# Two 64-row matmuls for the third input block's low pass, in the up-projection tiles of 512 columns

## The chip, the core and the metric

The kernel runs on one core of one Trainium2 chip. The metric is device time in microseconds (us), the median of several executions. Lower is better.

## The reference: what is computed

A gated recurrent attention runs over 4 batches, 8 heads and 768 positions of head size 40. Its output, 3072 rows of 320 values, goes through a gated feed-forward layer:

```python
x = np.ascontiguousarray(attn_out.transpose(0, 2, 1, 3)).reshape(B * S, H * D)   # 3072 x 320
gate = 1.0 / (1.0 + np.exp(-(x @ w_gate)))     # w_gate: 320 x 1536
val = x @ w_val                                # w_val:  320 x 1536
return (gate * val @ w_out).astype(np.float32) # w_out:  1536 x 320
```

The change sits in the two products `x @ w_gate` and `x @ w_val`, called the up-projection here.

## The kernel before

**The chunks.** The 768 positions are worked in six chunks of 128. A chunk holds 128 positions of each of the four batches, so 512 rows of `x`. In the kernel these are the columns of a transposed `x` with the 320 features on the partitions.

**High and low parts.** The matmuls run in the type fp32r, which keeps fewer bits than fp32. Each operand is therefore split into a high part (rounded to fp32r) and a low part (what is left): `xh` and `xl` for the input, `wh` and `wl` for the weights. A product is the sum of three passes: high times high, low weight times high input, high weight times low input.

**The three input blocks.** The 320 features make two blocks of 128 partitions and a third of 64. For the third block the kernel writes the 64 features twice, in partitions 0 to 63 and again in 64 to 127 (`twice`). Its weights lie in a tile `w2[n]`, n = 0 for the gate and 1 for the value: 64 partitions (`HP[n]`) hold the high part and the other 64 the low part. The high part of the gate is in partitions 0 to 63, that of the value in 64 to 127. One matmul of 128 rows with `w2[n]` then adds high and low weight times the input at once. It is done twice, with `xh` and with `xl`, for each of gate and value.

**A tile of the up-projection.** `ffn_up(n)` makes one tile: 128 of the 1536 output features, and either all 512 columns of the chunk (41 tiles) or 256 of them (62 tiles). It issues 16 matmuls, eight into the PSUM bank `pg0` (gate) and eight into `pg1` (value). The last two are the third block's passes with `xl`: first into `pg0`, then into `pg1`. In the text below they are called A and B. After that ScalarE takes tanh of `pg0` (line 811), VectorE multiplies with `pg1` (line 814), and two more operations (818, 822) split the product into `gh` and `gl`. The next tile's first matmul writes `pg0` again and so waits until the tanh has read it. `ffn_down` (line 833) multiplies `gh` and `gl` with the output weights into PSUM tiles `po`.

**The order of the work.** A long table of words written by hand, `ORDER`, sets the order in which every instruction is issued. The word `t27` issues the next of the 16 matmul steps of tile 27, `p26` the next down-projection matmul of tile 26, `a`, `b`, `s`, `c` and others steps of the attention. Each engine takes its instructions in the order issued.

**Where the matmul array is divided.** Most matmuls use the array whole, 128 rows by 128 columns. Two kinds do not. Line 599, `by_columns`, multiplies the score matrix with the values in four column strips of 32 (`av`, 64 instructions in a row for each batch of a chunk). Line 317 transposes gate values that lie in 32 partitions, and so uses 32 rows (`pt_h`, `pt_k`).

Of the kernel before, what the change touches and what calls it, by code (L numbers as in the profile page):

```python
# [178 lines left out]
def mlstm_then_gated_ffn_kernel(  # L179
# [13 lines left out]
    nc = tc.nc  # L193
    B, H, S, D = q.shape
    P = 128
    L = P
# [8 lines left out]
    def E(name, c=0):  # L205
        x = PARAM["eng"].get(name, "p")
        return nc.gpsimd if x == "p" else nc.vector
# [35 lines left out]
    def put(key, f, *args):  # L243
        todo.setdefault(key, []).append((f, args))
# [144 lines left out]
    wh, wl, w2 = [], [], []  # L389
# [7 lines left out]
    HP = (slice(0, 64), slice(64, P))  # L397
# [97 lines left out]
    xh, xl = {}, {}  # L495
# [286 lines left out]
    def ffn_up(n):  # L782
        c, j, t0, t1 = tiles[n]
        n0, n1 = t0 * L, t1 * L
        nt = n1 - n0
        u = (c, j, t0)
        fs = slice(j * P, (j + 1) * P)
        pg, sg = {}, []
        if n in PARAM['wllate']:
            order = [(x, i) for x in range(2) for i in (0, 2)] + [(0, 1), (1, 1)]  # L790
        else:
            order = [(x, i) for x in range(2) for i in (0, 1, 2)]

        def mm(x, w, y, a):
            first = x not in pg
            if first:
                pg[x] = ps_o.tile([P, NT], F32, tag=f"pg{x}", name=f"pg{x}_{c}_{j}_{t0}")[:, :nt]
            nc.tensor.matmul(pg[x], w[:, a, fs] if a < 2 else w[:, fs], y[c][:, a, n0:n1],  # L798
                             start=first, stop=a == 2 and y is xl)

        for x, i in order:
            w, y = ((wh, xh), (wl, xh), (wh, xl))[i]
            for a in range(2):
                put(f"t{n}", mm, x, w[x], y, a)
        for y in (xh, xl):
            for x in range(2):
                put(f"t{n}", mm, x, w2[x], y, 2)

        def tanh():
            sg.append(two.tile([P, NT], F32, tag="sg", name=f"sg_{c}_{j}_{t0}", bufs=1)[:, :nt])  # L810
            nc.scalar.activation(sg[0], pg[0], AF.Tanh, scale=0.5)  # L811

        def gate():
            nc.vector.scalar_tensor_tensor(sg[0], sg[0], 1.0, pg[1], ALU.add, ALU.mult)  # L814

        def high():
            gh[u] = two.tile([P, NT], F32R, tag="gh", name=f"gh_{c}_{j}_{t0}")
            nc.scalar.activation(gh[u][:, :nt], sg[0], AF.Copy)  # L818

        def low():  # L820
            gl[u] = two.tile([P, NT], F32R, tag="gl", name=f"gl_{c}_{j}_{t0}")
            E('gl0' if c == 0 else 'gl').tensor_tensor(gl[u][:, :nt], sg[0], gh[u][:, :nt].bitcast(F32), ALU.subtract)  # L822

        for key, f in (("ta", tanh), ("tg", gate), ("th", high), ("tl", low)):
            put(f"{key}{n}", f)
# [171 lines left out]
    for u in range(NU):  # L997
        c, b = divmod(u, B)
# [60 lines left out]
```

## Time and profile before

| | |
|---|---|
| median of 3 runs | 541.68 us (541.53 to 541.98) |
| the profiled execution | 541.76 us |
| its span, first to last instruction | 540.0 us |
| TensorE matmuls (PE) | busy 519.3 us, 4739 instructions |
| TensorE weight loads (PEld) | busy 469.3 us |
| VectorE (DVE) | busy 317.7 us |
| ScalarE (ACT) | busy 230.2 us |
| GpSimd (POOL) | busy 163.3 us |
| granted TensorE clock, mean | 0.99 |

PE and PEld are two sides of the same engine: every matmul is preceded by a load of its stationary operand, and the load can run while an earlier matmul streams. Matmuls overlap in the record: each row gives a start and a length that includes the pipeline, so the length of one (402 ns for 512 columns) is longer than the distance from its start to the next start. The distance between starts is what a matmul costs in a stream. In a timeline row such as `104.83 0.63 PE ... x2`, two matmuls stand in one row: the first starts at 104.83 us, and the end of the second is 0.63 us later. In a row of the chain of work, `310.43 3.26 PE pg L798 x14`, the second number is the time for which these 14 instructions were what the end waited for.

### The profile page before, as it was taken

Reading aid. Unit: us, or ns where it says so; the run is one execution under the profiler, and the core shown is the slowest. Engines: PE = TensorE matmul, PEld = TensorE weight load, DVE = VectorE, ACT = ScalarE, POOL = GpSimd, SP = SyncE. Lnnn points to the kernel's source line nnn. Section 1 sums busy time; section 2 is a strip of 40 time slices with the busy share of each in tenths; the row PEclk is TensorE's granted clock in tenths of the full one; section 3 lists DMA queues with packets and bytes.
Section 4 is the critical chain, followed back from the end, with each engine's and each line's share of the span. In section 5 each row is a group of like instructions: output and inputs, shape, how many; then the busy total and the mean of one; then the engine's idle time right before and its main releaser. Section 6 shows DMA issues by size and latency. Waiting matters only on the chain.

```text
span 540.0 us, 12183 instructions
## 1 busy us (share of the span) xinstructions
PE 519.3 (96%) x4739; PEld 469.3 (87%) x4739; DVE 317.7 (59%) x739; ACT 230.2 (43%) x581; POOL 163.3 (30%) x231
## 2 busy tenths in 40 slices
PE   8756999999999999999999999999999999999997
PEld 7545988888999999998888888888888888999996
DVE  5979798877655655545656645455744444543322
ACT  4676768563633443434333443243432422132322
POOL 5767667465330252040304341115210310000000
PEclk9879999999999999999999999999999999999999
DMA  9998877133596848377488385685287444000000
GB/s 196 222 258 201 220 202 184 60 85 74 143 190 174 195 99 169 78 203 152 106 182 166 74 219 146 149 193 126 58 215 185 105 107 120 25 26 1 25 1 24
DMA packets 131648, 72.41 MB, mean 134 GB/s; under 512 B 103112, under 2 KB 120776, under 8 KB 131592
## 3 DMA queue, kind: packets, MB, share of 16 engines
q1 hardware_dynamic: 130504, 71.39, 55.6%
q8 instruction: 37, 0.61, 0.5%
q10 hardware_dynamic: 1088, 0.26, 0.3%
q14 instruction: 19, 0.16, 0.1%
HBM read 56.95 MB, written 14.68 MB: 133 GB/s over the span
## 4 chain that ended last, share of the span: by engine, by line
PE 84%; DMA 6%; DVE 4%; SPq 3%; ACT 1%; issue 1%; POOL 0%; DVEq 0%; POOLq 0%; ACTq 0%
PE pg L798 48%; PE po L833 22%; PE av L599 3%; DMA qs<-scr 3%; PE pt L508 3%; PE s L629 2%; PE in L650 2%; PE cs L751 2%; PE s L624 1%; PE xt L719 1%; DMA st_o<-in_moe_w_out_dram 1%; DVE gl L822 1%; SPq L255 1%; DMA q<-in_q_dram 1%; DMA scr<-warm 1%
## 5 line engine op out<-in xcount | busy, mean ns | idle before, releaser
L798 PE MATMUL pg<-xh,wh 128*128 128x256 f32 (+1 forms) x412 | 112.3, 339 | 5.0 <-ACT sg L811 4.7
L811 ACT ACTIVATE sg<-pg 128x256 f32<-128x256 f32 (+1 forms) x103 | 48.2, 468 | 149.9 <-PE pg L798 146.8
L798 PE MATMUL pg<-xh,wl 128*128 128x256 f32 (+1 forms) x412 | 110.9, 336 | 0.0
L798 PE MATMUL pg<-xl,wh 128*128 128x256 f32 (+1 forms) x412 | 109.3, 335 | 0.0
L814 DVE SCALAR_TENSOR_TENSOR sg<-sg,pg 128x256 f32<-128x256 f32 (+1 forms) x103 | 54.0, 524 | 90.5 <-ACT sg L811 68.3
L833 PE MATMUL po<-oh,gl 128*128 128x320 f32 x288 | 90.8, 318 | 0.5 <-DVE gl L822 0.5
L833 PE MATMUL po<-oh,gh 128*128 128x320 f32 x288 | 91.0, 319 | 0.1
L833 PE MATMUL po<-ol,gh 128*128 128x320 f32 x288 | 90.6, 317 | 0.0
L822 DVE TENSOR_TENSOR gl<-sg,gh 128x256 fp32r<-128x256 f32 (+1 forms) x103 | 64.7, 628 | 27.6 <-ACT gh L818 27.4
L798 PEld LDWEIGHTS pg<-xh,wh 128*128 128x128 f32 x412 | 70.6, 191 | 10.9 <-ACT sg L811 6.6
L818 ACT ACTIVATE gh<-sg 128x256 fp32r<-128x256 f32 (+1 forms) x103 | 51.7, 502 | 58.3 <-DVE sg L814 55.7
L798 PEld LDWEIGHTS pg<-xl,wh 128*128 128x128 f32 x412 | 69.6, 191 | 4.7
L798 PEld LDWEIGHTS pg<-xh,wl 128*128 128x128 f32 x412 | 69.8, 191 | 4.4
L798 PE MATMUL pg<-xl,w 128*128 128x256 f32 (+1 forms) x206 | 58.5, 329 | 0.0
L833 PEld LDWEIGHTS po<-oh,gl 128*128 128x128 f32 x288 | 54.0, 188 | 3.9 <-DVE gl L822 0.9
L833 PEld LDWEIGHTS po<-oh,gh 128*128 128x128 f32 x288 | 54.3, 189 | 2.7 <-ACT gh L818 0.4
L833 PEld LDWEIGHTS po<-ol,gh 128*128 128x128 f32 x288 | 54.1, 188 | 2.9
L798 PE MATMUL pg<-xh,w 128*128 128x256 f32 (+1 forms) x206 | 53.3, 333 | 0.0
L702 POOL COPY x<-x 128x64 f32<-128x64 f32 x22 | 6.2, 280 | 153.8 <-DVE x L697 132.0
L635 DVE TENSOR_TENSOR d<-s,d 128x384 f32<-128x384 f32 (+1 forms) x66 | 32.9, 508 | 29.6 <-PE s L629 29.0
L367 POOL TENSOR_TENSOR d<-at,d 128x1024 f32<-128x1024 f32 x16 | 30.6, 1914 | 28.1 <-DMA d<-mscr 28.0
L798 PEld LDWEIGHTS pg<-xl,w 128*128 128x128 f32 x206 | 36.2, 189 | 2.2
(129 smaller groups left out, 776.4 us busy)
## 6 DMA issues: line engine op xcount, KB each, us to landing
d<-mscr SPq DMA_DIRECT2D x22, 512.0 KB
ks<-scr SPq DMA_DIRECT2D x16, 360.0 KB
qs<-scr SPq DMA_DIRECT2D x16, 360.0 KB
k<-in_k_dram SPq DMA_DIRECT2D x24, 160.0 KB
o<-in_o_gate_dram SPq DMA_DIRECT2D x24, 160.0 KB
v<-in_v_dram SPq DMA_DIRECT2D x24, 160.0 KB
st_o<-in_moe_w_out_dram SPq DMA_DIRECT2D x12, 320.0 KB
out_dram<-ob SPq DMA_DIRECT2D x24, 160.0 KB
```

The source lines that it names most:

```text
L367: E(arg).tensor_tensor(d, a, d, ALU.subtract)
L508: nc.tensor.transpose(pt[g][:r, x, :], t[u][:, h0 : h0 + nh, :].rearrange("p h d -> p (h d)"), ident)
L599: nc.tensor.matmul(dst[xs], lhs[:, xs], rhs, start=True, stop=True)
L629: nc.tensor.matmul(ps[g][:, m, :], ks[: 3 * D, 3 * m + g, :], qs[: 3 * D, 3 * m + g, :], start=True, stop=True)
L635: nc.vector.tensor_tensor(x, ps[g][:, :nh, :], x, ALU.mult)
L650: nc.tensor.matmul(pi[:, h0 : h0 + nh, :], qk[u][:r, g, :], cst[:r, b, g, : nh * DA], start=True, stop=True)
L798: nc.tensor.matmul(pg[x], w[:, a, fs] if a < 2 else w[:, fs], y[c][:, a, n0:n1], start=first, stop=a == 2 and y is xl)
L811: nc.scalar.activation(sg[0], pg[0], AF.Tanh, scale=0.5)
L814: nc.vector.scalar_tensor_tensor(sg[0], sg[0], 1.0, pg[1], ALU.add, ALU.mult)
L818: nc.scalar.activation(gh[u][:, :nt], sg[0], AF.Copy)
L822: E('gl0' if c == 0 else 'gl').tensor_tensor(gl[u][:, :nt], sg[0], gh[u][:, :nt].bitcast(F32), ALU.subtract)
L833: nc.tensor.matmul(po[t], g[c, j, t0][:, (t - t0) * P : (t - t0 + 1) * P], o[:, j, :], start=j == 0 and first, stop=j == NF - 1 and last)
```

## The change

In the 512-column tiles, and there alone, A and B become matmuls of 64 rows. A multiplies the high part of the gate's third block, which is in partitions 0 to 63, with the copy of `xl` in the same partitions. B does that for the value in partitions 64 to 127. Both are issued one behind the other at the step where A stood. The step where B stood issues nothing. The product of low weight and low input, which the 128-row matmuls had added too, is left out. Tiles of 256 columns stay as they were.

```diff
@@ ffn_up, mm(x, w, y, a): x is 0 for the gate and 1 for the value
             if first:
                 pg[x] = ps_o.tile([P, NT], F32, tag=f"pg{x}", name=f"pg{x}_{c}_{j}_{t0}")[:, :nt]
+            if a == 2 and y is xl and nt > 2 * L:
+                for z in range(2) if x == 0 else ():
+                    nc.tensor.matmul(pg[z], w2[z][HP[z], fs], y[c][HP[z], a, n0:n1], start=False, stop=True)
+                return
             nc.tensor.matmul(pg[x], w[:, a, fs] if a < 2 else w[:, fs], y[c][:, a, n0:n1],
                              start=first, stop=a == 2 and y is xl)
```

In the order of the instructions only TensorE's queue changes. In 20 of the 41 tiles A and B stood side by side before and still do; in 21 other work stood between them.

The first place is on TensorE in chunk 0, tile 5, at about 84 us of the span. `pg_0_5_0` with the larger number is `pg1`, with the smaller `pg0`; `w_100` and `w_103` are `w2[0]` and `w2[1]`, `xl_420` the low input. Before:

```order
L798 MATMUL pg_0_5_0_1257<-xh_398,w_103 128x512
L798 MATMUL pg_0_5_0_1223<-xl_420,w_100 128x512
L508 MATMUL pt_1_1_1291<-ident,q_1_560 80x128
L508 MATMUL pt_1_1_1291<-ident,k_1_717 80x128
L798 MATMUL pg_0_5_0_1257<-xl_420,w_103 128x512
L317 MATMUL pt_k__1295<-ident,gin 128x32 x4
```

With the change:

```order
L802 MATMUL pg_0_5_0_1257<-xh_398,w_103 128x512
L800 MATMUL pg_0_5_0_1223<-xl_420,w_100 128x512
L800 MATMUL pg_0_5_0_1257<-xl_420,w_103 128x512
L508 MATMUL pt_1_1_1292<-ident,q_1_560 80x128
L508 MATMUL pt_1_1_1292<-ident,k_1_717 80x128
L317 MATMUL pt_k__1295<-ident,gin 128x32 x4
```

B moved ahead of two transposes and stands behind A.

The second place is on TensorE in chunk 2, tile 11 of that chunk, at about 299 us, where the column strips of `av` follow. `s` are score matmuls, `po` the down-projection. Before:

```order
L798 MATMUL pg_2_11_0_4227<-xh_2567,w_103 128x512
L798 MATMUL pg_2_11_0_4213<-xl_2581,w_100 128x512
L629 MATMUL s_3_3_4256<-qs_3_4155,ks_3_4113 128x128 x2
L833 MATMUL po_2_3334<-oh,gh_10_0_4220 128x320
L798 MATMUL pg_2_11_0_4227<-xl_2581,w_103 128x512
L599 MATMUL av_3_4265<-v_3_3787,d_3_3785 32x41 x32
```

With the change:

```order
L802 MATMUL pg_2_11_0_4227<-xh_2567,w_103 128x512
L800 MATMUL pg_2_11_0_4213<-xl_2581,w_100 128x512
L800 MATMUL pg_2_11_0_4227<-xl_2581,w_103 128x512
L629 MATMUL s_3_3_4257<-qs_3_4155,ks_3_4113 128x128 x2
L833 MATMUL po_2_3334<-oh,gh_10_0_4220 128x320
L599 MATMUL av_3_4265<-v_3_3787,d_3_3785 32x41 x32
```

B moved ahead of two score matmuls and one down-projection matmul; the pair no longer touches the column strips. In one tile of the 41 (chunk 0, at about 105 us) the pair stands directly ahead of them, before and with the change.

## The prediction

> **What bounds the kernel now.** I read the page first, the busy times and the chain of work that ended last.
>
> ```profile
> span 540.0 us, 12183 instructions
> ...
> PE 519.3 (96%) x4739; PEld 469.3 (87%) x4739; DVE 317.7 (59%) x739; ACT 230.2 (43%) x581; POOL 163.3 (30%) x231
> ...
> PE 84%; DMA 6%; DVE 4%; SPq 3%; ACT 1%; issue 1%; POOL 0%; DVEq 0%; POOLq 0%; ACTq 0%
> PE pg L798 48%; PE po L833 22%; PE av L599 3%; DMA qs<-scr 3%; PE pt L508 3%; PE s L629 2%; PE in L650 2%; PE cs L751 2%; PE s L624 1%; PE xt L719 1%; DMA st_o<-in_moe_w_out_dram 1%; DVE gl L822 1%; SPq L255 1%; DMA q<-in_q_dram 1%; DMA scr<-warm 1%
> ```
>
> TensorE is busy 96% of the span, and line 798, which the change edits, is 48% of the chain. An average can hide a stage with another limit, so next come TensorE's busy time by stage and its waits there. The tiles of 512 columns all lie between 60 and 467 us.
>
> ```profile
> 60.00:130.00 70.00, 69.95 (x561) 60.70 (x563) 58.09 (x120) 44.32 (x112) 45.38 (x50) 1.00 0.48 126
> ...
> 240.00:467.00 227.00, 224.77 (x1990) 195.88 (x1989) 123.70 (x275) 78.34 (x170) 45.58 (x67) 1.00 0.60 139
> ```
>
> ```profile
> PE av L599 <- DVE d L635: 1.4, 2, 1.0
> PE s L629 <- DMA qs<-scr: 0.5, 1, 0.5
> PE xt L719 <- POOL v L258: 0.3, 1, 0.3
> ```
>
> The columns of the stages are length, then busy time of PE, PEld, DVE, ACT and POOL. PE is busy 69.95 of 70.00 us and 224.77 of 227.00. Its waits from 60 to 467 us sum to 2.2 us. So time added to or taken from TensorE's stream in these tiles goes into the end almost whole. Of the 2.2 us, the 1.4 follow scores that PE itself made and move with it; at most 0.8 us could absorb a delay.
>
> **What is removed.** The price of a 512-column matmul in a stream is the distance from start to start, read from a long run in the chain; how many there are, from the groups by form.
>
> ```profile
> 310.43 3.26 PE pg L798 x14
> ```
>
> ```profile
> L798 PE MATMUL pg<-xl,w 128*128 128x512 f32 x82 | 29.6, 401 | 0.0
> ```
>
> 3.26 / 14 = 0.233 us each, not the 401 ns of the record, which counts the pipeline twice. The 82 are A and B of 41 tiles. If A and B stream at the same time, one stream goes from each tile: 41 x 0.233 = 9.55 us.
>
> **What is added: dividing the array.** No matmul of 64 rows is in this trace, but two other divisions are: column strips of 32 (`av`) and strips of 32 rows (`pt_k`). The first is shown at tile 8 of chunk 0, TensorE's timeline:
>
> ```profile
> 104.36 0.63 PE L798 MATMUL pg<-xh,w 128*128 128x512 f32 x2
> 104.83 0.63 PE L798 MATMUL pg<-xl,w 128*128 128x512 f32 x2
> 105.39 0.82 PE L599 MATMUL av<-v,d 128*32 128x41 f32 x64
> 106.14 0.73 PE L798 MATMUL pg<-xh,wh 128*128 128x512 f32 x2
> 106.71 0.62 PE L798 MATMUL pg<-xh,wl 128*128 128x512 f32 x2
> ```
>
> Two streams from 104.83 would end at 105.30; the strips start at 105.39. Going in costs 0.09 us. For strips of rows:
>
> ```profile
> 58.69 0.31 PE L833 MATMUL po<-ol,gh 128*128 128x320 f32 x1
> 58.84 0.31 PE L833 MATMUL po<-oh,gl 128*128 128x320 f32 x1
> 59.08 0.24 PE L317 MATMUL pt_k__900<-ident,gin 32*128 32x32 f32 x1
> ```
>
> The `po` matmul starts 0.15 after the one ahead, the row strip 0.24 after `po`: again 0.09. The Trainium skill, "TensorEngine Tiling (Array Packing)", section Key Properties, says that changing the tiling mode drains TensorE, and this speaks against the change. The trace agrees for these two divisions; no run here shows 64 rows yet.
>
> The weight loads show where the time goes, and what else is lost. Timeline and tile view of the loads:
>
> ```profile
> 104.84 0.19 PEld L798 LDWEIGHTS pg<-xl,w 128*128 128x128 f32 x1
> 105.39 0.70 PEld L599 LDWEIGHTS av<-v,d 128*32 128x32 f32 x64 [0.36 <-PE pg L798]
> 106.14 0.30 PEld L798 LDWEIGHTS pg<-xh,wh 128*128 128x128 f32 x2
> ```
>
> ```profile
> L599 PEld LDWEIGHTS av<-v,d x1536: 106/109/120, 16.1 to 465.5; 128*32 128x32 f32 x192
> L599 PE MATMUL av<-v,d x1536: 197/200/225, 16.1 to 465.5; 128*32 128x41 f32 x192
> ```
>
> The load of the first strip waits 0.36 us for the matmul ahead, where loads otherwise run under the matmul ahead of theirs. Coming back is the same: the last `av` starts at 105.39 + 0.82 - 0.20 = 106.01, and the next load only at 106.14, 0.13 later, where neighbours are 0.01 apart. That is 0.12 for going out. After it the load is bare: the two matmuls from 106.14 take 0.57 to the next start instead of 2 x 0.233, so 0.10 for the load of 128 columns.
>
> Does a load of half the rows take half as long? Groups by form:
>
> ```profile
> L629 PEld LDWEIGHTS s<-qs,ks 120*128 120x128 f32 x128 | 20.5, 190 | 3.6 <-issue 1.2 <-PE pg L798 0.3
> L650 PEld LDWEIGHTS in<-cst,qk 80*128 80x128 f32 x40 | 6.1, 191 | 0.0
> L719 PEld LDWEIGHTS xt<-ident,x 128*128 128x128 f32 x72 | 8.9, 140 | 5.2 <-POOL x L697 2.4 <-DVE x L702 0.7 <-POOL v L258 0.5
> L317 PEld LDWEIGHTS pt_h__1302<-ident,gin 32*128 32x128 f32 x4 | 0.3, 137 | 0.0
> ```
>
> 80 rows take 191 ns and 120 rows 190; among transposes 32 rows take 137 and 128 rows 140. Rows do not matter.
>
> Now each unknown with its two ends:
>
> - Switch in and switch out. Lower end 0 (a half array that needs no pause; below zero is excluded, since streams already follow each other without a gap), upper end 0.12. I take 0.09, which both divisions show going in, behind matmuls as long as A and B. 41 tiles make 82 switches; the pair directly ahead of `av` shares one. 81 x 0.09 = 7.3 us.
> - Bare load of A. From 0 to 0.11 (the second load at 106.14 starts 0.30 - 0.19 = 0.11 after the first). I take 0.10, as for the whole array: 41 x 0.10 = 4.1 us.
> - Bare load behind B, shown for the whole array: 0.10, with 40 tiles (before `av` it is paid already): 4.0 us.
> - Start of B behind A. Lower end 0; upper end 0.233, a full stream. The 64 loads of column strips start (0.70 - 0.11) / 63 = 0.01 us apart and so run side by side. I take this 0.01 for row strips too: 0.4 us.
>
> What is moved is B, in 21 tiles, ahead of other TensorE work; nothing moves in another queue. The work passed is issued about a stream later. VectorE waits for some of it, and PE waited for VectorE's `d` only 1.4 us in all, so I cost this at nothing.
>
> **A cover that is nearly used up: the tanh.** The next tile's first matmul writes `pg0`, which the tanh must have read.
>
> ```profile
> 276.76 0.39 PE L798 MATMUL pg<-xl,w 128*128 128x512 f32 x1
> ...
> 277.19 0.60 ACT L811 ACTIVATE sg<-pg 128x512 f32<-128x512 f32 x1 [0.62 <-PE pg L798]
> ...
> 277.84 0.30 PEld L798 LDWEIGHTS pg<-xh,wh 128*128 128x128 f32 x2
> ...
> 277.96 0.40 PE L798 MATMUL pg<-xh,wh 128*128 128x512 f32 x1
> ```
>
> ```profile
> PEld pg L798 <- ACT sg L811: 0.7, 3, 0.3
> ```
>
> A starts at 276.76, the tanh ends at 277.79, the load that waited for it starts at 277.84, its matmul at 277.96. No slack is left in such a tile. By the timeline eleven tiles have at most 1.22 us from A to the next tile's first matmul. With the values above, the tanh comes 0.10 later against A's recorded start, and the next tile's first matmul -0.233 + 0.10 + 0.01 + 0.09 + 0.10 = 0.07 later: 0.03 short, eleven times, 0.3 us.
>
> **Sum.** 7.3 + 4.1 + 4.0 + 0.4 + 0.3 - 9.55 = +6.55 us, or +0.16 us a tile. The profiled execution took 541.76 us (1.76 beside its span of 540.0), the median is 541.68. 541.68 + 6.55 = 548.2 us.
>
> **The rivals.** Differences below 0.2%, about 1.1 us, are no change to a measurement of this kernel.
>
> 1. The halves need no pause, and all loads stay hidden: 41 x (0.01 - 0.233) = -9.1 us. The tanh gives back part: the next tile's first matmul would come 0.22 earlier with no slack in eleven tiles, some 2.5 us. The time is 535.1 us, faster. It is decided at 0.22 us of switches and loads a tile: below that the change gains. For it speaks that no 64-row matmul was seen, and that `av` runs strips side by side. Against it, both divisions that were seen pause. The packing that it hopes for stands in the Trainium skill, "TensorE: Matmul & The Clock Gate", section "Part 3: Packing small matmuls", which gives 3.07 times for four strips of 32 rows with 512 columns and a start 4 ns apart; the trace agrees on strips side by side (0.01 us), and no run here shows the gain without the pauses.
> 2. Pauses, but both loads run under them: 7.3 + 0.4 - 9.55 = -1.85, and the tanh gives back nearly all (0.13 in eleven tiles, less in others, about 1.7): 541.6 us, no change. Against it: the load at 106.14 was bare.
> 3. Only A's load is hidden: 6.55 - 4.1 = +2.45, 544.1 us. The short strips at 105.39 and 59.08 do not show a bare load clearly, since theirs are short.
> 4. The loads of A and B queue at 0.11 instead of running side by side: 41 x 0.10 = 4.0 more, 552.2 us. For it: whole loads behind a wait follow each other at 0.11. Against it: `av`'s strips, which are strips of columns.
> 5. The change does not do what it says: A and B stream one behind the other. 41 x 0.223 = 9.1 more, 557.4 us.
>
> **Chances.** The forecast 0.50; rivals in order 0.07, 0.04, 0.12, 0.19, 0.08. Rivals 1, 2 and 5 are left outside the range (0.19). Its low end is rival 3 with 0.6 of the 0.8 us absorbed, 543.5; its high end rival 4 with 0.12 for each of the 41 ways out, 1.2 more, 553.4. Faster: rival 1 and a quarter of rival 2, 0.08. No change: the rest of 2 and a corner of 3, 0.04. Slower: 0.88.
>
> **What would show it.** In the profile after, 82 matmuls of form 64*128; A's start 0.32 us behind a 512-column matmul ahead of it, not 0.23 (switch in); B's start 0.01 behind A, not 0.11 or 0.23; the next start 0.33 behind B, and the one behind that 0.10 late (bare load). I am wrong if loads appear under the matmul ahead of the pair, if A's recorded length is not about 0.10 more than 0.40, or if waits of line 798's loads for the tanh grow by microseconds.

## The result: 1.3% slower

| | median, us | runs | ratio to before, 95% |
|---|---|---|---|
| before | 541.61 | 541.38 to 541.98 | |
| with the change | 548.32 | 547.36 to 550.71 | 1.013 [1.0097, 1.0163] |
| with the change, run again | 548.54 (before beside it: 541.79) | 547.53 to 549.46 | 1.0125 [1.0109, 1.0142] |

The forecast was 548.2 us. The profiled execution of the change is the slowest of its four (550.71 us), which has to be kept in mind below. Its page:

```profile
span 549.0 us, 12188 instructions
...
PE 527.5 (96%) x4739; PEld 461.1 (84%) x4739; DVE 316.2 (58%) x739; ACT 230.8 (42%) x581; POOL 162.3 (30%) x231
...
PE 85%; DMA 6%; DVE 3%; ACT 3%; SPq 1%; issue 1%; POOL 0%; DVEq 0%; POOLq 0%; ACTq 0%
```

TensorE still sets the end, and the number of matmuls is the same. The busy time of the loads fell, because the loads of A and B now lie on top of each other, and still the kernel is longer. Groups by form, TensorE and its loads, show the 82 half matmuls:

```profile
L800 PE MATMUL pg<-xl,w 64*128 64x512 f32 x82 | 20.5, 496 | 0.0
```

```profile
L800 PEld LDWEIGHTS pg<-xl,w 64*128 64x128 f32 x82 | 7.6, 183 | 12.9 <-issue 12.8
```

The same loads before the change, those of the 256-column tiles among them:

```profile
L798 PEld LDWEIGHTS pg<-xl,w 128*128 128x128 f32 x206 | 36.2, 189 | 2.2
```

82 matmuls of 496 ns are busy for only 20.5 us together, where the 82 of before took 29.6: each pair is nearly one. The load of half the rows takes 183 ns where the whole array's took 189, and the loader now stands idle 12.9 us ahead of the pairs, 0.31 us for each of 41; before, 2.2 us stood ahead of all 206.

The same tile that the prediction showed, tile 8 of chunk 0, in TensorE's timeline and that of its loads:

```profile
106.33 0.63 PE L802 MATMUL pg<-xh,w 128*128 128x512 f32 x2
106.89 0.50 PE L800 MATMUL pg<-xl,w 64*128 64x512 f32 x2
107.31 0.82 PE L599 MATMUL av<-v,d 128*32 128x41 f32 x64
108.07 0.73 PE L802 MATMUL pg<-xh,wh 128*128 128x512 f32 x2
```

```profile
106.88 0.19 PEld L800 LDWEIGHTS pg<-xl,w 64*128 64x128 f32 x2 [0.37 <-issue]
107.31 0.69 PEld L599 LDWEIGHTS av<-v,d 128*32 128x32 f32 x64 [0.24 <-issue]
```

Two ordinary matmuls from 106.33 would end at 106.80; the pair starts at 106.89, so 0.09 for going in. Both matmuls of the pair stand in 0.50 us, which is the length of one, and both loads in 0.19: they run side by side. 0.50 is 0.10 more than the 0.39 to 0.40 of a matmul whose load was hidden: the bare load. The next start is 107.31, 0.42 behind the pair, which is 0.10 (bare load), 0.233 (stream) and 0.09 (going out). What follows then pays for its own load. An ordinary place behind a pair, from the second profile of the change:

```profile
268.75 0.63 PE L802 MATMUL pg<-xh,w 128*128 128x512 f32 x2
269.31 0.50 PE L800 MATMUL pg<-xl,w 64*128 64x512 f32 x2
269.74 0.41 PE L837 MATMUL po<-ol,gh 128*128 128x320 f32 x1
269.99 0.31 PE L837 MATMUL po<-oh,gl 128*128 128x320 f32 x1
270.14 0.31 PE L837 MATMUL po<-oh,gh 128*128 128x320 f32 x1
```

The `po` at 269.74 is 0.41 long and holds the next one back until 269.99, 0.25 later, where its followers are 0.15 apart: 0.10 for its load. From 268.75 to 269.99 it is 1.24 us. The same five steps before the change (four streams of 0.233 and one `po` of 0.147) take 1.08: 0.16 us longer, the forecast for one tile.

Where the extra time of the first profile lies is told by TensorE's waits over the span:

```profile
PE pt L508 <- DVE at L321: 3.0, 1, 3.0
...
PE s L629 <- DMA qs<-scr: 2.0, 2, 1.1
PE av L599 <- DVE d L635: 1.4, 2, 1.0
```

The first wait lies in the opening, ahead of all tiles of 512 columns, and was 1.2 us before. The scores waited 2.0 us for a DMA where it was 0.5 before. In the second profile the two are 1.6 and 1.1. So that profile gives the sum more cleanly. The `av` groups, the first and the last of which lie on either side of all these tiles, in the second profile:

```profile
span 546.8 us, 12188 instructions
...
L599 PE MATMUL av<-v,d x1536: 197/200/225, 15.6 to 472.4; 128*32 128x41 f32 x192
```

The last `av` starts at 472.4 us, where the row in the prediction has 465.5: 6.9 us later. The end of the span (546.8 against 540.0) is 6.8 us later. The 70 us behind the last 512-column tile add nothing.

The traces can also be laid side by side, since every matmul but B stands at the same place in the order. For each of the 41 tiles the time is taken from the start of the matmul ahead of A to the start of the third one behind B's old place (A and B not counted), and the same time of before is subtracted. The 41 differences add up to 6.39 us in the first profile and 6.41 us in the second, 0.16 for a tile. The rest of what the profiles are longer, 2.6 and 0.4 us, lies outside these stretches, mostly in waits in the opening and ahead of the scores. In the second profile the 21 tiles in which B moved are 0.16 us longer each, and so are the 20 in which it did not move, save the one directly ahead of `av`, which is 0.04 shorter. So the move of B is not what costs.

### The profile page after: what moved, and what is told of

Read it like the earlier page. It is cut to its first block, busy times and chain, and to the rows that moved or that the text cites. A ratio compares the mean times of both kernels' runs of the same rounds, so it can differ in the third digit from the quotient of the medians.

```text
span 549.0 us, 12188 instructions
## 1 busy us (share of the span) xinstructions
PE 527.5 (96%) x4739; PEld 461.1 (84%) x4739; DVE 316.2 (58%) x739; ACT 230.8 (42%) x581; POOL 162.3 (30%) x231
## 4 chain that ended last, share of the span: by engine, by line
PE 85%; DMA 6%; DVE 3%; ACT 3%; SPq 1%; issue 1%; POOL 0%; DVEq 0%; POOLq 0%; ACTq 0%
PE pg L802 44%; PE po L837 23%; PE pg L800 3%; DMA qs<-scr 3%; PE av L599 3%; PE pt L508 2%; PE s L629 2%; PE in L650 2%; PE s L624 2%; DMA st_o<-in_moe_w_out_dram 2%; PE cs L751 2%; PE xt L719 1%; PE mb L917 1%; DVE gl L826 1%; DMA st<-in_moe_w_val_dram 1%
## 5 line engine op out<-in xcount | busy, mean ns | idle before, releaser
L837 PE MATMUL po<-ol,gh 128*128 128x320 f32 x288 | 92.1, 322 | 0.0
L837 PE MATMUL po<-oh,gl 128*128 128x320 f32 x288 | 91.9, 322 | 0.1
L802 PEld LDWEIGHTS pg<-xh,w 128*128 128x128 f32 x206 | 34.8, 190 | 2.9
L383 POOL TENSOR_SCALAR_AFFINE_SELECT d<-d 128x1024 f32<-128x1024 f32 x22 | 26.3, 1200 | 30.1 <-ACT d L371 25.9
```

The costliest lines, as they stand in the source:

```text
L383: nc.gpsimd.affine_select(out=d, in_=d, pattern=[[0, H], [1, L]], compare_op=ALU.is_ge, fill=0.0, base=0, channel_multiplier=-1)
L837: nc.tensor.matmul(po[t], g[c, j, t0][:, (t - t0) * P : (t - t0 + 1) * P], o[:, j, :], start=j == 0 and first, stop=j == NF - 1 and last)
```

## The experiments

The theory: dividing the array costs a trip of 0.39 us (a pause of 0.09 and a bare load of 0.10 at each end), and the pair saves one stream of 0.233 us. The rivals: A and B do not really overlap and the trip is cheaper; the moved B is what costs; the loss goes with the number of columns. The edits of e1, e3, e4, e5 and e7 are shown against the change, those of e2, e6 and e8 against the kernel before. Ratios are against the kernel before, run beside each on the same chip (median 541.79 us for the first four, 542.22 for the next four, 541.84 for the last).

| run | median, us | ratio, 95% |
|---|---|---|
| e0_again, the change | 548.54 | 1.0125 [1.0109, 1.0142] |
| e1_same_half | 557.95 | 1.0299 [1.0282, 1.0317] |
| e2_drop_b_whole | 537.11 | 0.9907 [0.9887, 0.9927] |
| e3_drop_b_half | 548.69 | 1.0126 [1.0108, 1.0145] |
| e4_apart | 559.40 | 1.0315 [1.0291, 1.0338] |
| e5_all_tiles | 563.19 | 1.0389 [1.0365, 1.0412] |
| e6_trip_alone | 558.17 | 1.0292 [1.0271, 1.0313] |
| e7_two_pairs | 539.51 | 0.995 [0.9932, 0.9968] |
| e8_drop_a_whole | 534.87 | 0.9867 [0.9839, 0.9895] |

**e0_again: the change once more.**

> The changed kernel once more, since its first runs lay between 547.4 and 550.7 us. Theory (a trip into the half array costs 0.39 us in two pauses and two bare loads, and saves one stream of 0.233): 548.2 us, and the extra 2.5 us of the profiled run come from waits for DMAs, in the opening and ahead of the score matmuls, that are not there in every run. Rival (the moved B makes VectorE and the DMAs late): those waits are there every time and the time stays near 549 to 550 us.

548.54 us. The five runs reach from 547.53 to 549.46, so the 550.71 of the first profile is an edge, and the wait for `qs` is not the same in every run. B's move is not seen to make VectorE late: PE waited 1.4 us for `d` before and 1.4 in both profiles with the change.

**e1_same_half: do A and B overlap because they are in different halves?**

```diff
-                    nc.tensor.matmul(pg[z], w2[z][HP[z], fs], y[c][HP[z], a, n0:n1], start=False, stop=True)
+                    nc.tensor.matmul(pg[z], w2[z][HP[0], fs], y[c][HP[0], a, n0:n1], start=False, stop=True)
```

> B takes rows 0 to 63 like A (low instead of high weights of the value, so the value lacks one product), all else as in the change. Theory: two matmuls in the same half cannot stream at once, B starts a full stream of 0.233 us behind A instead of 0.003, 41 x 0.23 = 9.4 us more: 557.7 us. Rival (A and B of the change do not really stream at once, and the trip is cheaper than 0.39 us): no change, 548.3 us.

557.95 us, 9.4 above the change, as expected. The same place in its timeline:

```profile
106.56 0.73 PE L800 MATMUL pg<-xl,w 64*128 64x512 f32 x2
107.22 0.82 PE L599 MATMUL av<-v,d 128*32 128x41 f32 x64
```

The two matmuls of the pair take 0.73 us instead of 0.50: in one half they stand in line. The overlap in the change is real and is worth 0.23 us a tile.

**e3_drop_b_half: what does B cost beside A?**

```diff
-                for z in range(2) if x == 0 else ():
+                for z in range(1) if x == 0 else ():
...
-                             start=first, stop=a == 2 and y is xl)
+                             start=first, stop=a == 2 and (y is xl or nt > 2 * L and x == 1))
```

> A with 64 rows as in the change, B left out (the value lacks its low-input pass of the third block). Theory: B costs 0.003 us beside A, so leaving it out changes nothing: 548.2 us. Rival (A and B one behind the other): 41 x 0.233 = 9.5 us less than the change, 538.8 us.

548.69 us, no different from the change. B is free beside A. With e1 this settles it from both sides: the change does what it says, and the loss is in the trip.

**e6_trip_alone: the trip without a saving.**

```diff
+            if a == 2 and y is xl and nt > 2 * L and x == 0:
+                nc.tensor.matmul(pg[x][:, :32], w[HP[x], fs], y[c][HP[x], a, n0 : n0 + 32], start=False, stop=False)
             nc.tensor.matmul(pg[x], w[:, a, fs] if a < 2 else w[:, fs], y[c][:, a, n0:n1],
```

> The kernel before, with one 64-row matmul of 32 columns ahead of A in each 512-column tile (a product of 32 columns is added twice): the trip without any saving. Theory: 0.09 in, 0.10 bare load, 0.02 stream, 0.09 to 0.11 out, 0.10 bare load, so 0.40 to 0.42 us a tile, 41 x 0.41 = 16.8 us: 558.4 us. Rival (a short trip is cheap, the pair's cost lies in its two streams): 0.05 us a tile, 543.7 us.

558.17 us, 15.95 above before, so 15.95 / 41 = 0.39 us for each trip, with a stream of 32 columns in it. One of them in the timeline:

```profile
442.78 0.63 PE L800 MATMUL pg<-xh,w 128*128 128x512 f32 x2
443.34 0.28 PE L799 MATMUL pg<-xl,w 64*128 64x32 f32 x1
443.55 0.73 PE L800 MATMUL pg<-xl,w 128*128 128x512 f32 x2
444.11 0.31 PE L835 MATMUL po<-oh,gh 128*128 128x320 f32 x1
```

From 442.78 to 444.11 it is 1.33 us, where four streams are 0.93: 0.40 us for a matmul of 32 columns.

**e5_all_tiles: does the cost go with the columns?**

```diff
-            if a == 2 and y is xl and nt > 2 * L:
+            if a == 2 and y is xl:
```

> The pair in all 103 tiles, those of 256 columns too. Theory: the trip costs 0.39 us whatever the columns, and a 256-column stream saves only 0.12, so 62 more tiles cost 0.28 each, 17 us above the change: 565.5 us. Rival (the loss goes with the columns, since the half array streams slower): half of 0.16 us in each of the 62, 5 us more, 553.3 us.

563.19 us, 14.65 above the change: 0.24 us for each of the 62 tiles of 256 columns, more than the 0.16 of a 512-column tile and not half of it. The trip's price is fixed, and a shorter stream saves less. The expected 0.28 was 0.04 too high. Laid beside the trace of before, the median of the 62 tiles is 0.27 us longer, so the price holds; four tiles ahead of 60 us, where TensorE also waits for other engines, came to 0.41 us together instead of 1.1, and one directly ahead of `av` to 0.07. These come to some 0.9 us of the 2.4 that are missing to 17 us; the rest was not taken apart.

**e4_apart: must A and B be back to back?**

```diff
             if a == 2 and y is xl and nt > 2 * L:
-                for z in range(2) if x == 0 else ():
-                    nc.tensor.matmul(pg[z], w2[z][HP[z], fs], y[c][HP[z], a, n0:n1], start=False, stop=True)
+                nc.tensor.matmul(pg[x], w2[x][HP[x], fs], y[c][HP[x], a, n0:n1], start=False, stop=True)
                 return
```

> A and B are both 64 rows but stay at their old places: side by side in 20 of the 512-column tiles, with other work between them in 21. Theory (each trip into the half array costs 0.39 us): the 21 tiles make two trips and save no stream, 0.78 us over before instead of 0.16, so 21 x 0.62 = 13.0 us above the change: 561.3 us. Rival (B's move ahead of other work is what costs, trips are cheap): about halfway back to before, 545 us.

559.40 us. The rival is out: putting B back where it stood makes it slower by 10.9 us, since 21 tiles now make two trips. That is 0.52 us for each, and 0.62 was expected. Laid beside the trace of before, the 21 tiles are 0.74 us longer each, against the 0.78 of the theory and the 0.16 that they are longer with the change. That makes 12.1 of the 13.0 us that were expected; the other 1.2 us down to 10.9 lie outside these tiles, where for one TensorE waited 0.5 us for `qs` and not 1.1. Where a tile pays less than 0.78, a likely reason is that work beside the lone matmuls had bare loads already. The timeline of before shows it at the tile at 261 us, which is 0.69 us longer:

```profile
262.54 0.48 PE L798 MATMUL pg<-xl,w 128*128 128x512 f32 x1
262.85 0.49 PE L719 MATMUL xt<-ident,x 128*128 128x128 f32 x3
```

B starts at 262.54 behind six short matmuls and is 0.48 long, and the next start is 0.31 later, not 0.23: part of what a trip costs was lost there before. No run tested this by itself.

**e2_drop_b_whole and e8_drop_a_whole: the saving without a trip.** In e2 A is the whole-array matmul of before and B is left out; in e8 A is left out and B stays.

```diff
+            if a == 2 and y is xl and nt > 2 * L and x == 1:        # e8: x == 0
+                return
             nc.tensor.matmul(pg[x], w[:, a, fs] if a < 2 else w[:, fs], y[c][:, a, n0:n1],
-                             start=first, stop=a == 2 and y is xl)
+                             start=first, stop=a == 2 and (y is xl or nt > 2 * L and x == 1))   # e8: x == 0
```

> A as before the change with 128 rows, B left out in the 512-column tiles (the value lacks its low-input pass of the third block): the saving without any trip. Theory: 41 x 0.233 = 9.55 us less, of which the tanh ahead of the next tile's first matmul gives back some 2.5 us: 534.6 us, and waits of the loads of line 798 for the tanh rise from 0.7 us to about 2.5. Rival (the tanh has slack): 532.1 us and no such waits.

> As e2_drop_b_whole, but A is left out and B stays (the gate lacks its low-input pass of the third block). The same streams go, but the tanh can now start one stream earlier instead of the next tile one stream earlier. Theory (in e2 the tanh took back what was missing to 9.55 us): the full 41 x 0.233 = 9.55 us comes off, about 532.4 us, and the loads of line 798 wait for the tanh well under 1 us from 60 to 465 us. Rival (waits for the DMAs of the scores, or something else, took it back): 537 us again.

Both expectations missed by 2.5 us. e2 took 4.7 us off, not 7.1; e8 took 7.0 off, not 9.55. Loads waiting for the tanh from 60 to 465 us, in e2 and then in e8:

```profile
PEld pg L800 <- ACT sg L813: 3.3, 15, 0.3
```

```profile
PEld pg L800 <- ACT sg L813: 0.9, 4, 0.3
```

And TensorE's waits for the scores' DMA and for VectorE's `d` in the same stretch, e2 and then e8:

```profile
PE s L629 <- DMA qs<-scr: 2.6, 3, 2.1
PE av L599 <- DVE d L635: 1.1, 2, 0.9
```

```profile
PE s L629 <- DMA qs<-scr: 3.0, 4, 1.1
PE av L599 <- DVE d L635: 0.3, 1, 0.3
```

The tanh takes back what e8 wins over e2, 537.11 - 534.87 = 2.2 us, close to the 2.5 that the prediction gave it. The saving itself is there: laid beside the trace of before, each of the 20 places where A and B had stood side by side is 0.23 to 0.25 us shorter, in e2 and in e8. What is missing is partly more waiting for `qs`, 2.1 us in e2 and 2.5 in e8 above the 0.5 of before. But the wait for `d` fell, from 1.4 to 1.1 and 0.3. With the tanh (0.7 before) the waits grew by 4.4 us in e2 and by 1.6 in e8. Taken from 9.55 this leaves 5.2 and 8.0, where the medians show 4.7 and 7.0 (the profiled execution of e2 is 0.9 us above its median). So waits explain most of it, and some 1 us stays open. That a faster TensorE runs into the DMAs of the scores as its next limit is not shown. No run took that wait away, and it grew in a slower kernel too. In e1, 16 us above before, the row is:

```profile
PE s L629 <- DMA qs<-scr: 1.7, 2, 0.9
```

**e7_two_pairs: two streams saved on one trip.** The third block's pass with the high input becomes a pair too, so that four full streams become two paired ones.

```diff
-            if a == 2 and y is xl and nt > 2 * L:
-                for z in range(2) if x == 0 else ():
-                    nc.tensor.matmul(pg[z], w2[z][HP[z], fs], y[c][HP[z], a, n0:n1], start=False, stop=True)
+            if a == 2 and nt > 2 * L:
+                for p in (xh, xl) if y is xl and x == 0 else ():
+                    for z in range(2):
+                        nc.tensor.matmul(pg[z], w2[z][HP[z], fs], p[c][HP[z], a, n0:n1], start=False, stop=p is xl)
                 return
```

> Two pairs in one trip: the third block's passes with the high and with the low input both as pairs of 64 rows, four full streams replaced by two paired ones (the product of low weight and high input of the third block is left out). Theory: the second pair costs one stream, with its loads under the first pair, so the tile is 0.39 + 0.01 - 2 x 0.233 = -0.07 us against before, 41 x -0.07 = -2.7 us, of which the tanh takes some tenths: 539.2 us. Rival (the loads of the second pair are bare too, 0.10 more a tile): 543.2 us.

539.51 us, 2.7 below before, as expected. The timelines of one trip:

```profile
253.77 0.50 PE L801 MATMUL pg<-xh,w 64*128 64x512 f32 x2
254.11 0.40 PE L801 MATMUL pg<-xl,w 64*128 64x512 f32 x2
254.44 0.42 PE L838 MATMUL po<-ol,gh 128*128 128x320 f32 x1
```

```profile
253.77 0.19 PEld L801 LDWEIGHTS pg<-xh,w 64*128 64x128 f32 x2 [0.36 <-issue]
253.88 0.19 PEld L801 LDWEIGHTS pg<-xl,w 64*128 64x128 f32 x2
```

The second pair's loads start at 253.88, under the first pair's stream, and its matmuls are 0.40 long, not 0.50: within the half array loads are hidden again. The sign turns where the prediction put it: a trip of 0.39 us pays if it saves more than that in streams. Two streams (0.466) do, one (0.233) does not. This kernel leaves out the product of low weight and high input of the third block; with it as a third pair, three paired streams would stand for four full ones, and by the same sum only one stream would be saved again. So it is no version to keep, and none that beats the kernel before was found.

## Why the prediction was right

- **The bound.** TensorE's stream in the 512-column tiles sets the end. Right: the last `av` moved by 6.9 us, the end by 6.8.
- **The stream saved.** 0.233 us a tile. Right: e3 shows B free, e1 shows it worth 9.4 us in all, and at the 20 side-by-side places of e2 and e8 leaving out one stream takes 0.23 to 0.25 us off.
- **Switch in and out.** 0.09 each, taken from strips of other shapes. Right for 64 rows: the pair's start is 0.56 behind 106.33 instead of 0.47, and 0.42 to 0.43 from the pair to the next start leave 0.09 after the bare load and the stream.
- **The bare load of A and of what follows.** 0.10 each. Right: lengths 0.50 and 0.41 instead of 0.40 and 0.31. That the load goes with the columns and not the rows carried over as well (183 ns against 189).
- **B beside A.** Taken as 0.01 us from the column strips. Right: two matmuls in 0.50 us, two loads in 0.19. Rivals 4 and 5 fall with it, and rivals 2 and 3 with the lengths of A and of what follows.
- **No pause at all (rival 1).** Here a rule of the Trainium skill, "TensorEngine Tiling (Array Packing)", section Key Properties, that a change of tiling mode drains TensorE, was open for 64 rows. The trace agrees now: the pair starts 0.09 us late, and 12.8 us of the loader's idle time stand ahead of the pairs.
- **The tanh.** A few tenths were given to it. With the change the loads of line 802 wait little for it. The row of the second profile, from 60 to 475 us:

```profile
PEld pg L802 <- ACT sg L815: 0.8, 4, 0.3
```

It was 0.7 before, so 0.1 us and not 0.3. The 2.5 us that rival 1 lost to it came out as 2.2 between e2 and e8.
- **One sign was set wrong.** The next start was to be 0.33 us behind B. It is 0.42 to 0.43, because A's bare load lies between A's recorded start and its stream. The sum counts that load and the sign leaves it out.
- **What the prediction did not see.** In rival 1 the time without pauses was set at 535.1 us. e2, which removes the same stream without a trip, came to 537.1: longer waits for the scores' DMA, part of the gap, were not in that sum. Rival 2's own terms come to 541.5 us, not 541.6; nothing hangs on it.

The mechanism carried the number: the 41 places are 6.4 us longer, and the sum had 6.55. That 548.2 lies within 0.1 us of the first median is luck, since the runs of one kernel spread by 2 to 3 us here and the waits outside these places differ from run to run.

## What to carry to other kernels

Splitting the array so that two short contractions stream at once saves a stream, but each trip out of the whole array and back pays two pauses and two loads that nothing covers: here 0.39 us, against 0.233 us saved. Count trips first, then streams: at these prices a trip has to hold at least two saved streams of 512 columns, and its members must stand back to back. The price can be read beforehand, from any place in the trace where the array changes shape already: the distance between starts ahead of it and behind it, and the length of the first matmul after it.

## What was new about the hardware

A lone matmul of 32 columns and 64 rows in the middle of whole-array work costs 0.39 to 0.40 us (e6), more than one and a half full streams of 512 columns. Inside the half array, a second pair's loads are hidden under the first pair's streams and two pairs follow each other in 0.34 us, 0.10 of which is the first pair's load (e7), so the loss is at the two borders alone.
